# One paced load sequence, half-wide first stages, one PSUM ring and head-pair mask and norm in a sliding-window attention with a highway FFN

## The chip, the core and the metric

The kernel runs on one core of one Trainium2 chip. The metric is device time in microseconds (us) of one execution. Most executions agree within a per cent. Some run slower with a lower granted TensorE clock (the share of full clock that the profile's records show); they are marked as slow and left out of ratios. The span of a profile runs from its first to its last instruction; the device time of the same execution is some 1.7 us longer (213.98 us against 212.3 for the kernel before). Engines are PE (TensorE matmul), PEld (TensorE weight load), DVE (VectorE), ACT (ScalarE), POOL (GpSimd) and SP (SyncE). PSUM is the buffer that TensorE writes its results to; the program cuts it into tiles of one or two banks, a bank being 512 fp32 of each partition here. L394 is a line of the kernel in question, so the same step has another number in another kernel.

## The reference

```python
# q, k, v: (8 batches, 8 heads, 576 tokens, 64), fp32
scores = scale * q @ k.T
mask   = (rel >= 0) & (rel < 128)                 # rel = query position - key position
scores = where(mask, scores - slope[head] * abs(rel), -1e9)
attn   = softmax(scores)
x      = (attn @ v) as (4608 tokens, 512)
H = maximum(x @ w_h, 0)
T = 1 / (1 + exp(-(x @ w_t + b_t)))
out = T * H + (1 - T) * x                          # fp32
```

## The kernel before

Batches go in pairs ("duos", `m` = 0 to 3, two batches `r`). Each duo has two stages: "A" is query and key blocks of 128 tokens 0 and 1, "B" blocks 2, 3 and the tail of 64. For each head there are scores on TensorE, one exponential of 128x1024 on ScalarE, a mask on VectorE, then `pv` on TensorE and the division by the row sum ("norm") on VectorE. A finished stage of all eight heads gives four or five FFN blocks of 128 tokens. One block is: transpose `x`, `h = x @ w_h` (4 matmuls), `z = x @ w_t + b` (4 and a one-row bias matmul), `u = relu(h) - x` on VectorE, `tanh(z/2)` on ScalarE, `t = (tanh + 1)/2` on GpSimd, `u * t` on VectorE, `+ x` on GpSimd, and a store.

GpSimd issues all loads, which narrow fp32 to bf16 on the way. A planner orders all pieces by priorities before the program is emitted, so every engine has a fixed queue.

```python
RING = {"sc": 1, "tr": 2, "av": 2, "a": 1, "z": 1}     # PSUM buffers, one pool each
...
ones1 = cp.tile([1, P], BF16, name="ones1")
bT = cp.tile([1, DM], BF16, name="bT")
...
def mask(u):                                            # one head
    ...
    nc.vector.tensor_tensor(out=o, in0=o, in1=mk, op=ALU.mult)
...
def f_h(st, b):
    xt = XT[st, b]
    pa = ps_a.tile([P, DM], F32, name="pa")
    for c in range(NCK):
        nc.tensor.matmul(out=pa[:], lhsT=xt[:, c, :], rhs=wH[:, c, :], ...)
...
def f_z(st, b):
    xt = XT[st, b]
    pz = ps_z.tile([P, DM], F32, name="pz")
    for c in range(NCK):
        nc.tensor.matmul(out=pz[:], lhsT=xt[:, c, :], rhs=wT[:, c, :], ...)
    nc.tensor.matmul(out=pz[:], lhsT=ones1[:], rhs=bT[:], start=False, stop=True)
```

The softmax here doesn't subtract the row's maximum and nothing guards it: scores larger than these inputs give would overflow.

## Time and profile before

| | before |
|---|---|
| time, median of 3 runs | 212.35 us (212.16 to 212.93) |
| span of the profiled run | 212.3 us |
| TensorE busy | 173.5 us (82%) |
| VectorE, ScalarE, GpSimd busy | 142.4, 124.2, 119.5 us |
| read from HBM | 30.41 MB |

The page's slices are the place to start, since they show when an engine is busy and at which clock; the table of windows then gives numbers to a stretch, and the timeline of that stretch the order of waits.

### The profile page before, as it was taken

Reading aid. Unit: us, or ns where it says so; the run is one execution under the profiler, and the core shown is the slowest. Engines: PE = TensorE matmul, PEld = TensorE weight load, DVE = VectorE, ACT = ScalarE, POOL = GpSimd, SP = SyncE. Lnnn points to the kernel's source line nnn. Section 1 sums busy time; section 2 is a strip of 40 time slices with the busy share of each in tenths; the row PEclk is TensorE's granted clock in tenths of the full one; section 3 lists DMA queues with packets and bytes.
Section 4 is the critical chain, followed back from the end, with each engine's and each line's share of the span. In section 5 each row is a group of like instructions: output and inputs, shape, how many; then the busy total and the mean of one; then the engine's idle time right before and its main releaser. Section 6 shows DMA issues by size and latency. Waiting matters only on the chain.

```text
span 212.3 us, 5013 instructions
## 1 busy us (share of the span) xinstructions
PE 173.5 (82%) x2004; PEld 95.4 (45%) x2004; DVE 142.4 (67%) x308; ACT 124.2 (58%) x161; POOL 119.5 (56%) x137
## 2 busy tenths in 40 slices
PE   0547765995079679999999999999999999997940
PEld 0325443573045422556565445566453455543410
DVE  5626767570094164898886988897789979873550
ACT  2340355657023544889878868877878778824420
POOL 7993493429365395845333896543345564554662
PEclk9999999999555855999999999999999999999995
DMA  5599999999999999994223999322223333324244
GB/s 60 57 195 175 181 173 141 199 172 136 121 196 212 212 165 167 127 199 124 63 54 73 109 114 186 82 54 49 57 70 77 73 79 73 79 51 99 52 98 99
DMA packets 70135, 24.97 MB, mean 118 GB/s; under 512 B 48096, under 2 KB 65504, under 8 KB 70112
## 3 DMA queue, kind: packets, MB, share of 16 engines
q0 software_dynamic: 63328, 15.21, 90.9%
q1 hardware_dynamic: 6784, 9.45, 18.1%
q8 instruction: 15, 0.25, 0.5%
q14 instruction: 8, 0.07, 0.1%
HBM read 30.41 MB, written 9.44 MB: 188 GB/s over the span
## 4 chain that ended last, share of the span: by engine, by line
PE 57%; DMA 25%; POOL 10%; issue 2%; ACT 2%; DVE 1%; POOLq 1%; SPq 0%; ACTq 0%; DVEq 0%
DMA kl<-in_k_dram 19%; PE pz L381 14%; PE pa L364 13%; PE sc L274 8%; PE av L310 8%; DMA va<-in_v_dram 6%; PE pz L383 5%; PE pt L210 4%; PE pt L346 4%; POOL va L104 3%; POOL ql L83 2%; POOL kl L83 1%; POOL ot L403 1%; ACT pt L284 1%; POOL tri L142 1%
## 5 line engine op out<-in xcount | busy, mean ns | idle before, releaser
L284 ACT ACTIVATE pt<-sc,bias 128x1024 bf16<-128x1024 f32 x64 | 71.3, 1115 | 40.9 <-PE sc L274 40.7
L403 POOL TENSOR_TENSOR ot<-uu,x 128x512 f32<-128x512 bf16 x36 | 45.4, 1262 | 21.6 <-DVE uu L399 18.1
L295 DVE TENSOR_TENSOR pt<-pt,mk 128x1024 bf16<-128x1024 bf16 x64 | 49.1, 769 | 6.0 <-ACT pt L284 5.5
L394 POOL TENSOR_SCALAR tt<-tt 128x512 f16<-128x512 f16 x36 | 23.1, 641 | 37.6 <-ACT tt L390 34.7
L310 PE MATMUL av<-va,pt 128*128 128x65 bf16 (+1 forms) x576 | 33.2, 206 | 9.5 <-DVE pt L295 8.0
L364 PE MATMUL pa<-wH,xt 128*128 128x512 bf16 x144 | 39.6, 400 | 1.2 <-ACT xt L356 0.7
L381 PE MATMUL pz<-wT,xt 128*128 128x512 bf16 x144 | 39.8, 401 | 0.2 <-ACT tt L390 0.2
L310 PEld LDWEIGHTS <-pt 128*128 128x128 bf16 (+1 forms) x576 | 25.5, 105 | 23.4 <-DVE pt L295 8.9
L390 ACT ACTIVATE tt<-pz 128x512 f16<-128x512 f32 x36 | 21.6, 599 | 22.0 <-PE pz L383 20.4
L372 DVE SCALAR_TENSOR_TENSOR uu<-pa,x 128x512 bf16<-128x512 f32 x36 | 24.7, 686 | 14.1 <-PE pa L364 14.0
L274 PE MATMUL sc<-qt,kt 64*128 64x256 bf16 (+2 forms) x384 | 28.5, 258 | 5.1 <-ACT pt L284 3.4
L336 DVE TENSOR_TENSOR x<-av,rd 128x256 bf16<-128x256 f32 (+1 forms) x64 | 29.3, 458 | 2.2
L104 POOL DMA_DIRECT2D va<-in_v_dram x20 | 22.2, 1112 | 12.7 <-DMA kl<-in_k_dram 4.2
L399 DVE TENSOR_TENSOR uu<-uu,tt 128x512 bf16<-128x512 bf16 x36 | 16.1, 448 | 17.6 <-POOL tt L394 16.8
L356 ACT COPY xt<-pt 128x512 bf16<-128x512 bf16 x36 | 20.9, 583 | 6.3 <-PE pt L346 6.2
L335 DVE RECIPROCAL rd<-av 128x4 f32<-128x4 f32 (+1 forms) x64 | 11.7, 183 | 15.6 <-PE av L310 15.1
L274 PEld LDWEIGHTS <-kt 64*128 64x128 bf16 x384 | 13.7, 98 | 16.2 <-issue 11.5
L381 PEld LDWEIGHTS <-xt 128*128 128x128 bf16 x144 | 12.3, 101 | 14.4 <-issue 4.3
L346 PE MATMUL pt<-ident,x 128*128 128x128 bf16 x144 | 15.3, 231 | 3.7 <-DVE x L336 3.7
L364 PEld LDWEIGHTS <-xt 128*128 128x128 bf16 x144 | 12.3, 100 | 12.8 <-issue 3.6
L210 PE MATMUL pt<-ident,ql 128*64 128x128 bf16 x256 | 11.8, 244 | 6.9 <-POOL ident L127 5.0
L210 PE MATMUL pt<-ident,kl 128*64 128x128 bf16 x256 | 12.9, 256 | 3.9 <-DMA kl<-in_k_dram 2.2
(42 smaller groups left out, 123.1 us busy)
## 6 DMA issues: line engine op xcount, KB each, us to landing
out_dram<-ot SPq DMA_DIRECT2D x128, 64.0 KB, 1.7
va<-in_v_dram POOLq DMA_DIRECT2D x16, 256.0 KB, 9.3
ql<-in_q_dram POOLq DMA_DIRECT2D x3, 1024.0 KB, 15.6
kl<-in_k_dram POOLq DMA_DIRECT2D x3, 1024.0 KB, 18.1
out_dram<-ot SPq DMA_DIRECT2D x8, 128.0 KB, 2.3
ql<-in_q_dram POOLq DMA_DIRECT2D x2, 384.0 KB, 5.6
kl<-in_k_dram POOLq DMA_DIRECT2D x2, 384.0 KB, 7.9
qtl<-in_q_dram POOLq DMA_DIRECT2D x8, 64.0 KB, 16.5
```

What stands on the lines that cost most here:

```text
L104: nc.gpsimd.dma_start(out=VA[i][0:n, c, :, :, 0:D].rearrange("s r h d -> s (r h) d"), in_=v[2 * m : 2 * m + 2, :, c * P : c * P + n, :].re ...
L210: nc.tensor.transpose(out=pt[r * D : (r + 1) * D, hl * 512 + t * P : hl * 512 + (t + 1) * P], in_=L[:, r, 2 * hp + hl, t * D : (t + 1) * D ...
L274: nc.tensor.matmul(out=sc[:, r, off : off + w], lhsT=KT[i][rows, h, j * P : (j + 1) * P], rhs=rhs, start=True, stop=True,)
L284: nc.scalar.activation(out=pt[:], in_=SC.pop(u)[:], func=ACTF.Exp, bias=BIAS[:, h : h + 1], scale=scale,)
L295: nc.vector.tensor_tensor(out=o, in0=o, in1=mk, op=ALU.mult)
L310: nc.tensor.matmul(out=av[rows, g, :], lhsT=pt[:, r, off : off + w], rhs=va[:, j, r, h, :], start=n == 0, stop=n == len(terms) - 1,)
L336: nc.vector.tensor_tensor(out=x[:, 0:nb, h * D : (h + 1) * D], in0=av[:, 0:nb, 0:D], in1=rd[:, 0:nb].to_broadcast([P, nb, D]), op=ALU.mult,)
L346: nc.tensor.transpose(out=pt[:, c * P : (c + 1) * P], in_=X[st][:, b, c * P : (c + 1) * P], identity=ident[:],)
L364: nc.tensor.matmul(out=pa[:], lhsT=xt[:, c, :], rhs=wH[:, c, :], start=c == 0, stop=c == NCK - 1)
L372: nc.vector.scalar_tensor_tensor(out=uu[:], in0=pa[:], scalar=0.0, in1=X[st][:, b, :], op0=ALU.max, op1=ALU.subtract,)
L381: nc.tensor.matmul(out=pz[:], lhsT=xt[:, c, :], rhs=wT[:, c, :], start=c == 0, stop=False)
L403: nc.gpsimd.tensor_tensor(out=ot[:], in0=UU.pop((st, b))[:], in1=X[st][:, b, :], op=ALU.add)
```

## The change

The intent is to let the loads run as one paced sequence that matches the order in which data is needed, to start work on the first data earlier, to take TensorE's waits on single PSUM buffers away, and to spend less on VectorE.

```diff
+    ORDER = ("abcd", "AB", "AB", "AB")       # duo 0 in four half-wide stages
+    BUFS = {"ps": 4, ...}
-    RING = {"sc": 1, "tr": 2, "av": 2, "a": 1, "z": 1}
+    def ps_tile(dt=F32):                     # every PSUM tile: two banks, ring of four
+        return psp.tile([P, 2, 512 if dt == F32 else 1024], dt, name="ps")
...
-    bT = cp.tile([1, DM], BF16, name="bT")
+    bT = cp.tile([P, DM], BF16, name="bT")   # row 0 is the bias, the rest zero; ones1 alike
...
+    def load_wf():                           # w_h in fp32 by the sync queue, cast on ScalarE
...
     def mask(m, kind, g):                    # now a pair of heads, and so is norm
...
     def f_h(m, kind, b):
-        pa = ps_a.tile([P, DM], F32, name="pa")
+        az = ps_tile()                       # h in bank 0, z in bank 1 of one tile
...
+        if m == 0:
+            qk(0, 0); qk(0, 1); vv(0, 1); w_t, b_t; qk(1); vv(2, 3); tl(); vv(4)
+        else:
+            qk(); tl(); vv(0, 1, 2, 3, 4)
```

(The core of a diff of some 900 lines; the last six lines are written closer than in the kernel.) A half-wide stage covers one key block, so its exponentials are 128x512. The planner also models the loads' pace: in the program GpSimd's loads rotate through eight completion slots, so each waits for the load eight places before it.

## The prediction

> **What bounds the kernel now.** I read the page's slices first, to see where the engines are idle.
>
> ```profile
> PE   0547765995079679999999999999999999997940
> PEclk9999999999555855999999999999999999999995
> DMA  5599999999999999994223999322223333324244
> GB/s 60 57 195 175 181 173 141 199 172 136 121 196 212 212 165 167 127 199 124 63 54 73 109 114 186 82 54 49 57 70 77 73 79 73 79 51 99 52 98 99
> ```
>
> A slice is 5.3 us. From slice 17 on (about 90 us) TensorE is full at full clock; before that it is part idle, and from slice 10 to 15 its clock is halved. The DMA rows are the reverse: full from 10 to 95 us, light afterwards. So there are two regimes: a load-bound first 90 us, and a TensorE-bound rest. The table of ten-microsecond windows puts numbers on it:
>
> ```profile
> 40.00:50.00 10.00, 10.00 (x183) 6.62 (x181) 6.28 (x13) 6.31 (x8) 3.66 (x4) 1.00 2.24 173
> 50.00:60.00 10.00, 1.66 (x34) 1.22 (x31) 1.85 (x5) 2.74 (x3) 5.64 (x8) 0.70 3.48 135
> 60.00:70.00 10.00, 9.54 (x91) 5.19 (x90) 6.12 (x12) 4.13 (x5) 5.77 (x6) 0.50 1.55 208
> 100.00:110.00 10.00, 10.00 (x164) 6.37 (x162) 8.47 (x18) 8.12 (x11) 3.92 (x5) 1.00 0.24 56
> ```
>
> The columns after the width are busy PE, PEld, DVE, ACT, POOL, then clock. All compute collapses at 50 to 60 us. The timeline there says why:
>
> ```profile
> 53.98 0.68 POOL L95 DMA_DIRECT2D ktl<-in_k_dram  x1 [0.87 <-DMA va<-in_v_dram]
> 56.74 0.68 POOL L95 DMA_DIRECT2D ktl<-in_k_dram  x1 [2.08 <-DMA va<-in_v_dram]
> 57.45 0.63 POOL L394 TENSOR_SCALAR tt<-tt 128x512 f16<-128x512 f16 x1
> 58.12 0.42 DVE L399 TENSOR_TENSOR uu<-uu,tt 128x512 bf16<-128x512 bf16 x1 [11.36 <-POOL tt L394]
> 58.46 0.68 DVE L295 TENSOR_TENSOR pt<-pt,mk 128x1024 bf16<-128x1024 bf16 x1
> 59.20 0.82 PE L310 MATMUL av<-va,pt 128*128 128x65 bf16 x11 [6.65 <-DVE pt L295]
> ```
>
> GpSimd issues the loads and also computes one step of the FFN (L394). It sits before a load until an earlier load has landed; L394 stands behind that in its queue, VectorE waits 11.36 us for L394, the mask behind it is late, and TensorE waits 6.65 us for the mask and comes back at half clock. The waits list has the same again at 72 us, where GpSimd waits 6.0 us for a `kl` load. In the full-clock regime I read the timeline of the last blocks, where TensorE does nothing but FFN:
>
> ```profile
> 195.93 1.03 PE L381 MATMUL pz<-wT,xt 128*128 128x512 bf16 x4
> 196.89 0.39 PE L383 MATMUL pz<-bT,ones 1*128 1x512 bf16 x1
> 197.21 0.40 PE L346 MATMUL pt<-ident,x 128*128 128x128 bf16 x4
> 197.44 1.03 PE L364 MATMUL pa<-wH,xt 128*128 128x512 bf16 x4
> 198.31 1.03 PE L381 MATMUL pz<-wT,xt 128*128 128x512 bf16 x4
> ```
>
> Start to start: L364 0.87 us (4 x 0.215), L381 0.96, bias row L383 0.32, transposes 0.23, together 2.38 us a block. L381 and L383 would take 0.86 + 0.215 if they streamed like L364; the one-row bias matmul costs 0.10 us ahead of it and 0.10 after it.
>
> **What the Trainium skill says.** "DMA: Bandwidth & Descriptors", Specifications, gives an HBM limit of about 358 GB/s for a core. The trace agrees: loads narrow fp32 to bf16, so the 173 GB/s written at 40 to 50 us are some 346 GB/s read, and I take the loads as saturated. "TensorE: Matmul & The Clock Gate", Part 1, says that an idle window of some 3.4 us halves the clock; the trace agrees with its 0.50 after the 6.65 us gap (that page's few microseconds of warming don't fit: it stayed cold until about 84 us, over 20 us).[...] "VectorE: DVE Perf Modes", the section on the TRN2 errata, says that the cost of an operation is a fixed part plus elements; its (N+151)/0.96 at two elements a cycle gives 691 ns for the 1024-wide mask, and the timeline has 0.68 to 0.69.
>
> **The change part by part.**
>
> *Loads.* The bytes are the same (30.4 MB read). Order and pace change: first duo by token halves, 8 issues of about 0.78 us from 1.3 us on, so the identity is only made at about 8 us instead of 5 and the first exponential comes at 13 us instead of 10.8 (a loss of 2 to 3 us, but early work waits for `va` anyway). Then second halves, w_t, v, tails; w_h goes by the sync queue with a 2 us cast on ScalarE. Ahead of the first `va` there are 2.1 + 1.05 + 2.1 + 1.05 MB, and it is 0.5 MB: 6.8 MB at 350 GB/s = 19.5 us, plus 2 us start and 2 us landing: 23.5 us (before: 24.25). The rest of duo 0 brings 9.2 MB, 27 to 30 us; duo 1's q and k are 4.2 MB, so 42 us. In before duo 1's last q/k transposes ran at 67 us, because TensorE's queue stood behind the waits above.
>
> *Half-wide first stages.* FFN no longer waits for all of tokens 0 to 255 of eight heads: stage a ends after block 0. In before the first L364 is at 37.9 us; now attention of a and b is waiting masked when `va` lands, and norm of a (4 pairs at 0.6 us) lets FFN start at 27 us. Cost: 32 exponentials of about 0.65 us for 16 of 1.115, +3 us of ScalarE in the first 40 us; twice as many, narrower transposes, +4 us of TensorE.
>
> *Bias with 128 rows of zeros.* Removes 0.2 us a block x 36 = 7.2 us of TensorE.
>
> *Pairs.* Masks: 48 at 0.69 become 24 at (1024+151)/0.96 = 1.22 us: 33.1 to 29.3, 3.8 us saved. Norm: 0.424 and 0.492 us for 256 and 320 elements, slope 1.06 ns, so 512 and 640 take 0.70 and 0.83: per duo 7.3 to 6.1, and 8 reciprocals of 0.18 fewer: 2.6 x 3 = 8 us. VectorE loses 12 of 142 us. It isn't the bound, so this only gives slack.
>
> *PSUM ring.* Scores, transposes, av and FFN tiles share four two-bank slots in place of seven separate buffers. It lets score tiles run ahead of the exponential (in before one `sc` buffer makes a 1.87 us cycle: 0.76 + 1.11), but a slot held by a late tanh or norm stops TensorE whatever comes next. Per duo 47 tiles in 36 us: each may live 4 x 0.77 = 3.1 us; h + z + tanh is 0.86 + 1.08 + 0.6 = 2.5 us at least. I charge 5 to 7% of TensorE's time.
>
> *Sum.* In before, 90 to 180 us holds 22 FFN blocks (88 L364 matmuls), 244 of 384 score matmuls (2.54 duos) and 224 q/k transposes (1.75 duos). With 21.3 us of FFN and 5.3 of transposes a duo, attention is (90 - 52 - 9.3)/2.54 = 11.3, and a duo 37.9 us; four 151 us. So the first 90 us did 37 us worth of work. After: four duos at 36.0, plus 4, 148 us. By 27 us some 13 us of it are done (transposes and scores of the first stages); the other 135 at 93% take 145: TensorE ends at 172. The last block's tanh, two GpSimd and one VectorE steps and the store took 8.5 us behind the last matmul (203.8 to 212.3), and stay. 180.5 us. A second way: duo 1's first exponential at 42.5, three duos at 37.8, then the 28 us from the last exponential to the end, of which eight blocks get 0.2 us shorter plus the better overlap, 25: 181.
>
> **Rivals.**
>
> *GpSimd still blocks FFN.* The built order puts the first `t` steps of the FFN between loads of duo 1, and the later ones behind loads that can only be issued when `ql` and `kl` of duo 1 have landed (some 36 and 42 us). If only three blocks pass before 43 us, TensorE idles, cools, and 8 to 10 us are lost: 190.
>
> *ScalarE becomes the bound.* Per duo: 16 x 1.115 + 9 x (0.583 + 0.6) + 4 x 1.01 + 0.59 = 33.1 us, against 36.0 on TensorE. Near enough to queue, which together with the ring gives a period of 39 to 40: 187. Against it: ScalarE sits at 8.2 tenths in before, with waits of 40.7 us for scores that the ring removes.
>
> *Nothing is lost to the ring.* Period 36: 173 to 175.
>
> *The load-bound phase just moves.* If halves and pacing leave the queue empty, duo 1 comes at 50 instead of 42 us: 188. To be no faster at all, the first 90 us would have to stay as they are.
>
> **Range and chances.** Predicted 180 us. The range of 171 to 192 runs from a frictionless ring to one of the first two rivals in full. For only 208 or more two rivals must add up and the clock must stay low as well: faster 0.93, within 2% 0.04, slower 0.03.
>
> **What would show it.** Right: first FFN matmul near 27 us, duo 1's first exponential near 42 us, no TensorE gap of over 3 us after 30 us and full clock from about 35 us, bias matmuls spaced 0.215 us, pair masks of 1.22 us, PE busy near 165 us or less. Wrong: GpSimd load issues waiting on earlier loads with VectorE behind them at 30 to 60 us; TensorE waiting for tanh or norm (the ring) over 10% of 60 to 160 us; a halved clock after 50 us; ScalarE over 95% busy.

## The result and the profile after

| | before | after |
|---|---|---|
| time, median of the first comparison | 212.64 us (4 runs) | 191.03 us (188.49 to 193.32, 4 runs) |
| ratio of fast runs | | 0.8904 (95% interval 0.8813 to 0.8995) |
| time, repeated later beside the experiments | 213.01 us (11 runs) | 190.9 us (190.04 to 194.48) |
| ratio of fast runs | | 0.9002 (0.895 to 0.9055) |
| TensorE, VectorE busy in the profiled run | 173.5, 142.4 us | 152.3, 136.9 us |
| span of the profiled run | 212.3 us | 188.6 us |

A ratio here is the mean time of one kernel's fast runs over that of the other's of the same rounds, so it is not quite the ratio of the medians. The kernel is about 10% faster. The time lies inside the predicted range, but 11 us above the predicted 180.

The page's slices after the change, 4.7 us each:

```profile
PE   0287769897899888899978889998988899979900
PEclk9999999999999999999999999999999999999995
DMA  4999999999999999999999912043030222433453
GB/s 164 219 183 190 162 128 133 196 190 148 185 178 225 223 197 175 139 200 225 229 172 188 103 41 76 20 99 98 20 87 26 59 70 56 103 81 86 111 128 94
```

The clock row no longer drops: the halved stretch of before is gone. But TensorE is no longer at 9 throughout the second half either; it is between 7 and 9 nearly everywhere. The windows after, with the same columns as those of before (busy PE, PEld, DVE, ACT, POOL, then the clock), show the exchange:

```profile
40.00:50.00 10.00, 8.54 (x167) 5.65 (x167) 8.34 (x16) 6.64 (x11) 7.90 (x8) 1.00 2.45 167
50.00:60.00 10.00, 8.98 (x128) 5.67 (x131) 7.55 (x16) 7.58 (x10) 9.17 (x11) 1.00 1.62 195
60.00:70.00 10.00, 8.88 (x118) 5.49 (x121) 7.70 (x12) 8.00 (x12) 6.57 (x7) 1.00 1.56 217
100.00:110.00 10.00, 8.36 (x105) 5.30 (x104) 7.50 (x12) 7.32 (x11) 3.70 (x5) 1.00 1.26 120
```

At 50 to 60 us TensorE is busy for 8.98 us instead of 1.66 us. At 100 to 110 us it is busy for 8.36 us, where it was full before. So the change wins its time in the load-bound part and gives some back in the part that TensorE bounded.

What it gives back shows in the list of waits (waiting engine and line, releaser, total us, times, longest):

```profile
ACT tt L415 <- DVE uu L400: 38.9, 34, 2.5
DVE uu L400 <- PE ps L410: 26.3, 29, 1.9
```

The times are those of waits that this releaser ended. L415 is the tanh of `z`, L400 is `u` from `h`, L410 is `z`'s bias row. Tanh needs nothing from `u`, and `u` needs nothing from `z`. They wait for each other because `h` and `z` now share one tile, and the program orders accesses by tile: `u` waits until the last write of `z` is done, and tanh waits until `u` has read. The timeline of one block shows what comes of it:

```profile
124.31 0.38 PE L410 MATMUL ps<-bT,ones 128*128 128x512 bf16 x1
...
124.79 0.69 DVE L400 SCALAR_TENSOR_TENSOR uu<-ps,x 128x512 bf16<-128x512 f32 x1 [0.62 <-PE ps L410]
...
125.52 0.60 ACT L415 ACTIVATE tt<-ps 128x512 f16<-128x512 f32 x1 [0.41 <-DVE uu L400]
...
126.17 0.40 PE L299 MATMUL ps<-qt,kt 64*128 64x256 bf16 x4 [0.20 <-ACT tt L415]
```

The bias row is done, then 0.69 us of `u`, then 0.60 us of tanh, and only then do the scores L299 of another head get the slot. From 60 to 160 us TensorE's own list puts three groups of waits, 5.2 us in all, on tanh. The FFN tile lives 0.86 + 1.08 + some 0.1 + 0.69 + 0.60 us and the small gaps, so about 3.4 us in place of the 2.5 us that the prediction took as its least.

The bias row itself is as predicted. From the last blocks:

```profile
170.07 1.03 PE L408 MATMUL ps<-wT,xt 128*128 128x512 bf16 x4
170.93 0.38 PE L410 MATMUL ps<-bT,ones 128*128 128x512 bf16 x1
171.15 1.03 PE L394 MATMUL ps<-wH,xt 128*128 128x512 bf16 x4
```

From L408 to L410 are 0.86 us and from L410 to the next L394 0.22 us, where before they were 0.96 and 0.32.

The first part of the time is late against the prediction. This is the timeline from the landing of duo 1's `kl` to duo 1's first exponential (some lines of other work left out):

```profile
45.07 0.64 PE L248 MATMUL ps<-ident,kl 128*64 128x128 bf16 x16 [0.50 <-DMA kl<-in_k_dram]
45.90 1.01 ACT L273 COPY kt<-ps 128x1024 bf16<-128x1024 bf16 x1
...
48.23 0.64 PE L248 MATMUL ps<-ident,ql 128*64 128x128 bf16 x16
48.70 0.61 PE L248 MATMUL ps<-ident,kl 128*64 128x128 bf16 x16
...
49.24 0.39 PE L299 MATMUL ps<-qt,kt 64*128 64x256 bf16 x4
...
50.98 1.12 ACT L314 ACTIVATE pt<-ps,bias 128x1024 bf16<-128x1024 f32 x1
```

`kl` lands at 45.0 us, not 42. Then TensorE's queue has other work and the second pair of transposes before the first scores (L299, 64x256), and the first exponential of duo 1 starts at 50.98 us, not 42.5.

### The profile page after: what moved, and what is told of

It is laid out like the page before. It is cut to its first block, busy times and chain, and to the rows that moved or that the text cites. A ratio compares the mean times of both kernels' runs of the same rounds, so it can differ in the third digit from the quotient of the medians.

```text
span 188.6 us, 5196 instructions
## 1 busy us (share of the span) xinstructions
PE 152.3 (81%) x2108; PEld 96.1 (51%) x2132; DVE 136.9 (73%) x238; ACT 124.8 (66%) x178; POOL 122.0 (65%) x138
## 4 chain that ended last, share of the span: by engine, by line
PE 30%; DMA 19%; DVE 12%; ACT 12%; issue 11%; POOL 11%; SPq 1%; POOLq 1%; ACTq 0%; DVEq 0%
PE ps L394 11%; PE ps L408 10%; DMA kl<-in_k_dram 9%; DMA va<-in_v_dram 8%; DVE uu L400 7%; ACT pt L314 4%; ACT xt L386 4%; POOL ot L429 4%; DMA out_dram<-ot 3%; PE ps L410 3%; PE ps L248 2%; PE ps L347 2%; DVE pt L324 2%; ACT tt L415 2%; POOL ql L101 2%
## 5 line engine op out<-in xcount | busy, mean ns | idle before, releaser
L314 ACT ACTIVATE pt<-ps,bias 128x1024 bf16<-128x1024 f32 (+1 forms) x80 | 71.9, 951 | 6.2 <-PE ps L299 6.2
L429 POOL TENSOR_TENSOR ot<-uu,x 128x512 f32<-128x512 bf16 x36 | 46.7, 1297 | 22.9 <-DVE uu L424 22.8
L415 ACT ACTIVATE tt<-ps 128x512 f16<-128x512 f32 x36 | 21.5, 597 | 39.0 <-DVE uu L400 38.9
L400 DVE SCALAR_TENSOR_TENSOR uu<-ps,x 128x512 bf16<-128x512 f32 x36 | 24.9, 691 | 29.8 <-PE ps L410 26.3
L324 DVE TENSOR_TENSOR pt<-pt,mk 128x2048 bf16<-128x2048 bf16 (+1 forms) x40 | 43.7, 1099 | 0.7 <-ACT pt L314 0.7
L394 PE MATMUL ps<-wH,xt 128*128 128x512 bf16 x122 | 36.4, 384 | 4.2 <-ACT kt L273 0.6
L408 PE MATMUL ps<-wT,xt 128*128 128x512 bf16 x143 | 36.9, 379 | 0.1
L299 PE MATMUL ps<-qt,kt 64*128 64x256 bf16 (+2 forms) x384 | 27.1, 250 | 6.4 <-ACT tt L415 3.9
L347 PE MATMUL ps<-va,pt 128*128 128x65 bf16 (+1 forms) x576 | 24.9, 198 | 3.7 <-ACT pt L314 1.9
L364 DVE TENSOR_TENSOR x<-ps,rd 128x256 bf16<-128x256 f32 (+3 forms) x40 | 25.5, 638 | 1.4
L408 PEld LDWEIGHTS <-xt 128*128 128x128 bf16 x144 | 14.1, 98 | 17.2 <-issue 0.3
L394 PEld LDWEIGHTS <-xt 128*128 128x128 bf16 x144 | 12.7, 98 | 16.0 <-issue 4.6
L386 ACT COPY xt<-ps 128x512 bf16<-128x512 bf16 x36 | 20.5, 590 | 0.2 <-PE ps L378 0.2
L299 PEld LDWEIGHTS <-kt 64*128 64x128 bf16 x384 | 13.8, 96 | 12.8 <-issue 6.1
L378 PE MATMUL ps<-ident,x 128*128 128x128 bf16 x144 | 14.2, 224 | 2.9 <-ACT tt L415 2.0
```

The costliest lines, as they stand in the source:

```text
L299: nc.tensor.matmul(out=sc[:, r, o + off : o + off + w_], lhsT=KT[i][rows, h, j * P : (j + 1) * P], rhs=rhs, start=True, stop=True,)
L314: nc.scalar.activation(out=PT[m, kind, h // 2][:, h % 2], in_=SC[m, kind, h][:, :, o : o + W], func=ACTF.Exp, bias=BIAS[:, h : h + 1], sca ...
L324: nc.vector.tensor_tensor(out=o, in0=o, in1=mk.to_broadcast([P, 2, rep, W]), op=ALU.mult,)
L347: nc.tensor.matmul(out=av[rows, hl, n * (D + 1) : (n + 1) * (D + 1)], lhsT=pt[:, hl, r, off : off + (D if narrow else P)], rhs=va[:, j, r, ...
L364: nc.vector.tensor_tensor(out=x.rearrange("p b (h d) -> p h b d", h=2), in0=av[:, :, :, 0:D], in1=rd[:, :, 0:nb].to_broadcast([P, 2, nb, D ...
L386: nc.scalar.copy(out=xt[:], in_=TR[m, kind, b][:, 0, 0:512].rearrange("p (c n) -> p c n", c=NCK))
```

## The experiments

All were built from the changed kernel, with the kernel before timed on the same chip in the same rounds. The ratio to before is the common yardstick: 0.9002 for the changed kernel. One hundredth of ratio is 2.1 us. Differences in us below are those of ratios times 212 us, and with the widths of two intervals they are good to some 2 us. The yardstick is open by as much again: the changed kernel was timed twice, with 0.8904 and 0.9002, and not beside the runs from e4_order on. In e1_split, e2_ring3, e4_order, e7_wide, e8_mix, e13_mix0 and e14_first the planner also makes the order of the queues anew, so some part of what they show can be order; in e3_bias1, e5_extra, e6_heads and e10_less the order stays. Two theories stood at the outset. Theory A: TensorE's work and the PSUM ring set the end. Theory B: the moment when duo 1's q and k are there sets it.

**r0_after**, no edit, the yardstick.

> The changed kernel again, on the chip of the next three, as their yardstick. 188 to 193 us as in its four runs so far; it also shows how far it scatters from run to run (before scatters by 0.6%, this one by 2.6%).

Measured: 190.9 us, ratio 0.9002. In its profile the first exponential of duo 1 is at 51.63 us, the last exponential starts at 160.3 us, and the span is 189.3 us.

**e1_split**: `h` and `z` get a one-bank PSUM tile each, and the ring goes from four slots to three to make room.

```diff
-    "ps": 4,
+    "ps": 3, "a": 1, "z": 1,
-        az = ps_tile()
+        az = psa.tile([P, DM], F32, name="pa")      # and psz for z
```

> FFN's two products get a one-bank PSUM tile each (as in the kernel before), the ring of two-bank slots shrinks from 4 to 3. Theory A (the shared two-bank FFN tile makes u wait for z and tanh wait for u, which holds a ring slot some 0.7 us longer and stops TensorE, 7.2 us of waits from 60 to 160 us): the waits of tanh for u (38.9 us) and of u for the bias row (26.3 us) vanish, and 4 to 6 us are gained, about 185 us. Theory B (the shortfall is duo 1's late start at 51 us, set by its k load landing at 45 us): the waits vanish too, but the time stays within 1.5 us of the changed kernel.

Measured: 193.41 us, ratio 0.9112 (0.9051 to 0.9172). The false waits were gone, the end behind the last exponential was 3 us shorter, but duo 1 started at 56.85 us, with the clock at 0.82 between 40 and 50 us. Two things had been changed at once, so it decides nothing by itself.

**e2_ring3**: only the size of the ring is edited (and the planner, which knows it, orders the queues anew).

```diff
-    "ps": 4,
+    "ps": 3,
```

> The ring has 3 slots of two banks in place of 4, nothing else changes; the control of e1. Theory A (slots are short): each tile may live 3 x 0.77 = 2.3 us instead of 3.1, less than the FFN tile's 3.5 us, so 8 to 20 us slower, 198 to 210 us. Theory B (slots are not what limits): within 3 us of the changed kernel.

Measured: 221.52 us, ratio 1.045 (1.0388 to 1.0512), 31 us longer than with four slots and slower than before. The window table for 60 to 160 us:

```profile
60.00:160.00 100.00, 78.62 (x1083) 50.61 (x1098) 63.42 (x100) 65.15 (x82) 49.64 (x50) 0.97 0.99 111
```

TensorE is busy for 78.6 of 100 us. With the FFN's tile in the ring, three slots are far too few, worse than the 8 to 20 us expected. With the same three slots, e1_split is 28 us faster, so giving the FFN's tile two banks of its own, outside the ring, is worth about that much when slots are short.

**e3_bias1**: the one-row bias again.

```diff
-        nc.tensor.matmul(out=az[:, 1, :], lhsT=ones1[:], rhs=bT[:], start=False, stop=True)
+        nc.tensor.matmul(out=az[:, 1, :], lhsT=ones1[0:1, :], rhs=bT[0:1, :], start=False, stop=True)
```

> The bias matmul reads one row again instead of 128 rows of which 127 are zero; undoes that part alone. By the prediction 0.2 us of TensorE for each of 36 blocks: if TensorE is what limits, 5 to 7 us slower than the changed kernel (about 196 us); if TensorE's idle 10% absorbs it, under 2 us.

Measured: 196.83 us, ratio 0.9206 (0.9131 to 0.9281), so 4.3 us longer, of the 7.2 us of TensorE that the 128 rows promised.

**e4_order**: duo 1's q and k are issued ahead of duo 0's tails and last v.

```diff
-            node(key, "POOL", cost, pl + n_, emit, deps, land=land, n=n)
+            late = m == 0 and (key[0] == "tl" or key == ("v", 0, 4))
+            node(key, "POOL", cost, 0.5 * T + 0.01 * n_ if late else pl + n_, emit, deps, land=land, n=n)
```

(and three lines in the planner that keep the order of the rest)

> Duo 1's q and k are issued ahead of duo 0's tails and last v (0.79 MB, some 2.5 us of loading). Theory B (the arrival of duo 1's q and k sets the end, 51.6 + 110 + 28 us): duo 1's first exponential comes 2 to 4 us earlier, near 48, and the whole gets 2 to 4 us shorter, ratio near 0.886. Theory A (TensorE's work and the ring set the end, wherever duo 1 starts): the start may move, the time stays within 1 us of the changed kernel's or gets longer, because duo 0's last stage and its FFN blocks come later; ratio 0.90 or more.

Measured: 199.1 us, ratio 0.938 (0.9299 to 0.9462), 8 us longer. Duo 1's `kl` landed at about 39 us, 6 us earlier, yet its first exponential came at 56.66 us, 5 us later. Data that is there early is of no use when duo 0's last stage, which stands ahead in TensorE's queue, is late: its tails, put later by the edit, made TensorE wait 1.79 us for `ktl` at 44 us. The timeline of that stage shows something else:

```profile
46.76 4.05 DVE L324 TENSOR_TENSOR pt<-pt,mk 128x1024 bf16<-128x1024 bf16 x1 [1.28 <-ACT pt L314]
46.82 1.22 POOL L419 TENSOR_SCALAR tt<-tt 128x512 f16<-128x512 f16 x2
48.00 2.26 POOL L429 TENSOR_TENSOR ot<-uu,x 128x512 f32<-128x512 bf16 x2
```

A mask that takes 0.68 us elsewhere took 4.05 us, and it ended 0.5 us after four GpSimd instructions in a row had ended. TensorE waited 2.23 us for it. Its clock was 0.50 from 48 to 56 us, and had begun to fall before that wait (0.78 at 46 to 48 us). "SBUF — State Buffer", section "SBUF: two separate sides", in the Trainium skill says that VectorE and GpSimd share a pair of ports under an exclusive lock, held for the whole instruction. That fits these lines, and the account of VectorE's time below has more of it from the changed kernel's trace. With a late stage, a blocked mask and a cold clock in one run, e4_order doesn't decide between the theories.

**e5_extra**: two loads of 1 MB that nobody reads, in front of duo 1's q and k.

```diff
+        if m == 0 and c in (2, 3):
+            nc.gpsimd.dma_start(
+                out=wX[:], in_=(moe_w_h, moe_w_t)[c - 2].rearrange("(c p) n -> p c n", p=P))
```

> The opposite: two loads of 1 MB each (w_h and w_t again, into a tile that nothing reads) are put behind duo 0's v of blocks 2 and 3, nothing else moves in any queue. Theory B: at 312 GB/s the 2.1 MB make everything behind them 6.7 us later, duo 1's first exponential at 57 to 58 and the whole 5 to 7 us longer, ratio 0.925 to 0.933. Theory A: TensorE makes up for most of it out of duo 0's FFN backlog; at most 2 us longer, ratio under 0.91.

Measured: 198.54 us, ratio 0.9401 (0.9328 to 0.9473), 8.5 us longer. Its profile (of a run marked slow, span 198.1 us) has TensorE waiting for duo 1's data:

```profile
50.94 1.06 PE L252 MATMUL ps<-ident,kl 128*64 128x128 bf16 x16 [2.95 <-DMA kl<-in_k_dram]
...
58.89 2.13 ACT L318 ACTIVATE pt<-ps,bias 128x1024 bf16<-128x1024 f32 x2
```

`kl` comes about 6 us later, the first exponential 7.3 us later. Later data costs its full delay, and the clock, which was at 0.50 or 0.51 from 50 to 56 us in this run, may have cost the rest: 8.5 us is more than the 5 to 7 of theory B. Theory A as put there, with TensorE making up for the delay, failed this test.

**e6_heads**: mask and norm by single heads again, two instructions in the place of one.

```diff
+        for hl in range(2):
+            o = PT[m, kind, g][:, hl].rearrange("p r (j w) -> p (r j) w", w=W)
...
```

> Mask and norm by single heads again, two instructions in place of each one, at the same places of the queue. Prediction on record (only slack): VectorE gets 11 to 13 us busier, the time stays within 1 us, ratio 0.897 to 0.905. Rival (VectorE is in the loop that holds the PSUM slots and the probabilities): 3 to 6 us longer, ratio 0.915 to 0.93.

Measured: 194.09 us, ratio 0.921 (0.9154 to 0.9266), 4.4 us longer. VectorE was 14 us busier (149.1 us against 135.2). The rival is right: VectorE isn't just slack.

**e7_wide**: duo 0 with the two wide stages of the other duos.

```diff
-    ORDER = ("abcd", "AB", "AB", "AB")
+    ORDER = ("AB", "AB", "AB", "AB")
-        return (0, 1) if ORDER[m][0] == "a" else (None,)
+        return (0, 1) if m == 0 else (None,)
```

> Duo 0 with the two full-wide stages of the other duos; its loads still come by halves. First FFN matmul near 36 in place of 29 us. Prediction's sum (work that is not done before 30 us is added at the end): 4 to 7 us longer, ratio 0.92 to 0.935. Theory B (only duo 1's start counts): duo 1's first exponential within 1.5 us of 51.6, and the time 0 to 2 us longer or even shorter, since 16 exponentials of 0.69 us fewer are needed; ratio 0.895 to 0.91.

Measured: 197.1 us, ratio 0.9349 (0.9294 to 0.9403), 7.4 us longer. The first FFN matmul came at 42.8 us instead of 28.4, TensorE was busy for 6.00 us at 30 to 40 us instead of 8.99, and duo 1 started at 53.2 us. Theory B, by which only that start counts, expected 0 to 2 us. The half-wide stages are a real part of the gain.

**e8_mix**: the same 16 KB of PSUM cut in another way. Scores, q/k transposes and `av` have a ring of three two-bank slots; the FFN's x transposes, `h` and `z` have two one-bank slots.

```diff
-    "ps": 4,
+    "ps": 3, "pf1": 2,
+    def pf_tile(dt=F32):
+        return pfp.tile([P, 512 if dt == F32 else 1024], dt, name="pf")
-        az = ps_tile()                      # h and z in one tile
+        az = pf_tile()                      # one for h, another for z, another for x's transpose
```

> Scores, q/k transposes and av keep a ring of three two-bank slots; the FFN's x transposes, h and z get two one-bank slots of their own (the same 16 KB of PSUM), order made anew by the same rules. The false waits between h and z go, and the FFN no longer holds a slot that scores or av want. If the ring was what TensorE's 10 per cent of idle time came from (prediction's charge of 5 to 7 per cent): 4 to 8 us shorter than the changed kernel, ratio 0.86 to 0.88, mostly in shorter duos or a shorter end. If it is the loads and the order alone: within 2 us, ratio 0.89 to 0.91.

Measured: 184.71 us (183.53 to 186.49), ratio 0.8718 (0.8667 to 0.8769), correct, 6.0 us faster than the changed kernel. Duo 1 starts at 51.61 us, which is where it started with the old layout. The windows of 60 to 160 us, first of the changed kernel (r0_after), then of this one:

```profile
60.00:160.00 100.00, 90.35 (x1251) 58.13 (x1264) 76.56 (x120) 78.23 (x102) 60.83 (x60) 1.00 1.02 120
```

```profile
60.00:160.00 100.00, 93.77 (x1305) 57.56 (x1319) 86.30 (x131) 81.16 (x104) 65.18 (x65) 1.00 1.10 129
```

TensorE's idle time falls from 9.65 to 6.23 us, and more instructions fit in the same 100 us. TensorE's longest group of waits for tanh, in the changed kernel (r0_after) and here:

```profile
PE ps L299 <- ACT tt L415: 3.7, 9, 0.5
```

```profile
PE pf L399 <- ACT tt L421: 0.5, 1, 0.5
```

The gain lies in the duos: from duo 1's first to the last exponential they take 33.8 us each instead of 36.2. The waits of the FFN are now for what it needs, tanh for `z` (L416) and `u` for `h` (L399):

```profile
ACT tt L421 <- PE pf L416: 23.7, 22, 2.2
...
DVE uu L405 <- PE pf L399: 10.8, 11, 2.2
```

**e10_less**: 1.7 MB fewer in front of duo 1's q and k. Its output is wrong, which doesn't matter for the time.

```diff
+        nc.scalar.copy(out=wT[:].rearrange("p c n -> p (c n)"), in_=w_stage())   # w_t isn't loaded
+        nr = 1 if m == 0 and c >= 2 else 2                                       # half of three v blocks
```

> Wrong result on purpose. The counterpart of e5_extra: w_t is not loaded (ScalarE casts w_h twice, one 2 KB load stays in its place) and duo 0's last three v loads bring one of two batch rows (the rest is set to one); 1.7 MB fewer ahead of duo 1's q and k, the order of every queue unchanged. If the arrival of the first 13 MB sets duo 1's start and with it the end (slope of e5_extra: 7.6 us for 2.1 MB): duo 1's first exponential at 46 to 47 and the whole 4 to 6 us shorter, ratio 0.87 to 0.882. If the time only follows delays and earlier data is eaten by work of duo 0 that still has to be done: at most 2 us shorter, ratio 0.89 to 0.90.

Measured: 188.26 us, ratio 0.8908 (0.8845 to 0.8972), 2 us shorter, and duo 1 started at 48.88 us, 2.75 us earlier. The timeline, with L249 the transposes of duo 1:

```profile
42.31 0.38 PE L411 MATMUL ps<-bT,ones 128*128 128x512 bf16 x1
42.62 0.64 PE L249 MATMUL ps<-ident,kl 128*64 128x128 bf16 x16
```

No wait for `kl` stands beside the transposes any more. They come when the FFN block before them in the queue is done. Theory B, which by and large held for delays, fails for earlier data: behind the data limit lies the work of duo 0, less than 3 us away. The end did move about as far as the start (the profiled spans are 186.5 and 189.3 us), so this run speaks about the data, not about the start.

**e13_mix0**: e8_mix with the planner's priorities searched again for that layout.

```diff
-    LOOKS = {"PE": 70, "ACT": 0, "DVE": 109, "POOL": 178, "SP": 159}
+    LOOKS = {'PE': 367, 'ACT': 28, 'DVE': 402, 'POOL': 69, 'SP': 2813}
...
```

(and the twenty shifts of priority in the same way)

> A try at a better version: the PSUM layout of e8_mix with the priorities of the order chosen again for it (the changed kernel's were chosen for one ring of four). 2 to 4 us shorter than e8_mix if order is worth anything there, ratio 0.85 to 0.87; equal to it otherwise.

Measured: 186.55 us, ratio 0.8809 (0.8753 to 0.8864). A miss: it wasn't faster than e8_mix. But with two quite different orders this layout was 4 to 6 us faster than the changed kernel, which speaks for the layout, not the order, as the source of the gain; the old layout with a new order wasn't run.

**e14_first**: only the order, duo 1's first two scores and exponentials moved forward.

```diff
+                up = 8 * T if (m, kind, g) == (1, "A", 0) else 0.0
-                        node(tk, "PE", C[0] * len(hs), tg + (hl - 1.3) * U,
+                        node(tk, "PE", C[0] * len(hs), tg + (hl - 1.3) * U - up,
-                    node(("exp", m, kind, h), "ACT", C[1], tg + (hl - 1.2) * U,
+                    node(("exp", m, kind, h), "ACT", C[1], tg + (hl - 1.2) * U - up,
```

> Only the order: the scores and exponentials of duo 1's first two heads are given a higher priority, so that TensorE takes them before duo 1's second pair of transposes and an FFN block. Duo 1's first exponential comes about 3.5 us earlier, near 48. If the start of duo 1 as such sets the end (all three runs so far that moved it moved the end by the same amount): 3 to 4 us shorter, ratio 0.88 to 0.89. If that start is only where one sees how much of the work before it is done: the time stays within 2 us of the changed kernel's, ratio 0.893 to 0.912.

Measured: 193.47 us, ratio 0.9095 (0.9046 to 0.9144). Duo 1's first exponential came at 49.88 us, 1.75 us earlier and less early than planned, and the whole got 2 us longer, not shorter. After a wait of 1.63 us for a norm TensorE's clock was 0.53 at 44 to 46 us, and it was low again at 50 to 54 us, so part of that is the clock. An earlier start of duo 1 as such brought nothing; because of the clock it is no clean proof that it can't.

## Why the prediction was right or wrong

**Right: two regimes, and GpSimd as the cause of the hole at 50 to 60 us.** The hole and the half clock went away together, and VectorE's waits for GpSimd's `t` step fell from 16.8 to 1.2 us. From 27 to 180 us the list of waits of the changed kernel has no wait of TensorE longer than 0.8 us, and the clock is 1.00 all the while. The first rival, GpSimd blocking the FFN as before, did not come true. Which part of the change closed the hole is not shown: no run puts the old load sequence back alone. The half-wide stages aren't needed for it, since e7_wide has the clock at 1.00 without them. One reading was wrong: before's clock did not stay low until 84 us. It was back at 1.00 at 72 to 74 us and fell again when TensorE was busy for only 0.80 and 0.51 us of two windows of 2 us.

**Right: bias, sizes and first stages.** The bias row's spacing, the pair mask of 1.22 us, the norms of 0.69 and 0.83 us and the first `va` (22.8 us against 23.5) are as worked out. The first FFN matmul came at 29.2 us against 27. e7_wide shows that the half-wide stages are needed for it, and e3_bias1 puts 4.3 us on the bias.

**Wrong: "duo 1's q and k are 4.2 MB, so 42 us".** The 13.4 MB up to there landed at 45.0 us; over some 43 us of loading that is 311 GB/s, not 350. The rate was not one rate: at 36 to 40 us, with q and k under way, the windows have 198 GB/s written, 396 read; at 22.8 to 32.0 us, with v and the tails under way, 129 written, 258 read. Those are read in runs of 64 fp32 values and had been counted at the full rate. "DMA: Bandwidth & Descriptors", Specifications, asks for transfers of at least 512 B for the line rate; these runs of 256 B agree with it, and the prediction didn't apply it. It isn't all: the rate fell from 156 to 119 GB/s written in the course of those loads, which is unexplained. At 350 GB/s the 2.4 MB of these 9.2 us would have taken 6.8 us, so they cost 2.4 us.

**Wrong: the second way's use of that time.** "Duo 1's first exponential at 42.5, three duos at 37.8, then 25" treats the start of duo 1 as a clock from which the rest is counted. Measured, from start to start of exponentials as there, were 51.0, three times 36.2 and 29.0 us, which is 188.6: 8.5 us more, 4.7 less and 4.0 more. It looks as if the late start were the whole miss, and the rival "duo 1 comes at 50 instead of 42 us: 188" hits the time. But e8_mix ends 6 us earlier with the same start, e7_wide starts 1.6 us later and ends 7.4 us later, and with 1.7 MB fewer to load only 2 us come back. Only a delay passed through in full (e5_extra). The rival had the right time for a reason that the runs don't bear out: between 27 and 60 us TensorE was busy for 29.5 of 33 us in the changed kernel, so the late duo 1 was mostly other work done first.

**The sum, term by term.** The first way was 27 + 145 + 8.5 us, with 135 us of TensorE work and 10 us of idle time in the middle. In the profiled run it is 27 + 152.3 + 9.3. In the 152.3 us TensorE is busy for 29.5 + 90.3 + 18.3 = 138.1 us and idle for 14.2. So the miss of 8.1 us in the span is 3.1 us of work, 4.2 us of idle time and 0.8 us at the end. Of the idle time, 3.5 us fall before 60 us and 9.75 us between 60 and 160 us. The 0.8 us at the end is the false wait once more: the last block's tanh waited for `u`, which takes 0.69 us; in e8_mix, without it, the end behind the last matmul takes 8.5 us. What the additional 3.1 us of busy time are made of was not separated; ends of matmuls are modelled in these records. (The sum is one of spans. The time is 1.7 us longer than the span, and the median time 0.7 us longer than that of the profiled run: with them the miss is the 10.5 us from 180.5 to 191.0.)

**Mis-sized: the ring term.** "h + z + tanh is 0.86 + 1.08 + 0.6 = 2.5 us at least" failed because `u` stands in the chain by two false waits, of `u` for `z` and of tanh for `u`: a tile lives about 3.4 us, longer than the 3.1 us of average that four slots allow. The charge of 5 to 7% became 9.75% idle between 60 and 160 us, of which the waits list puts 5.2 us on tanh. e8_mix, which gives the FFN its own slots, takes 6 us back. How much of that is the false dependency and how much the FFN's occupancy of slots was not separated: e1_split took away the first and part of the second, but lost it at duo 1's start.

**Wrong: "this only gives slack".** Undoing the pairs costs 4.4 us. VectorE stands in both chains that hold PSUM slots, through `u` and through the norm, which is the likely way; why 14 us of VectorE time turn into 4.4 us was not followed instruction by instruction. VectorE's busy time fell by 5.5 us between before and after, not by 12. The saving itself came: all masks together fell from 49.1 to 43.7 us, norms with their reciprocals from 41.0 to 33.3. But the 36 products `u * t` rose from 16.1 to 21.0 us. The changed kernel's timeline shows how:

```profile
179.46 1.15 POOL L429 TENSOR_TENSOR ot<-uu,x 128x512 f32<-128x512 bf16 x1
180.02 0.87 DVE L424 TENSOR_TENSOR uu<-uu,tt 128x512 bf16<-128x512 bf16 x1
```

The product ends 0.28 us after GpSimd's addition has ended. Eleven of the 36 products start while a GpSimd instruction of the FFN is running; they take 0.55 to 1.37 us, and every one ends 0.27 to 0.29 us after that instruction. The other 25 take 0.41 to 0.43 us. In before only 2 of 36 start so. That is how blocking for a whole GpSimd instruction, as on the page named at e4_order, would look; the remaining 2.7 us were not taken apart.

**The rival of ScalarE as the bound** found no support: ScalarE was busy for 6.6 to 8.0 us of 10 in the windows shown, and for at most 8.8 in the other windows of ten.

The fastest version is e8_mix, 184.7 us.

## What to carry to other kernels

A shared ring of PSUM slots is paid for by its longest-lived tile, so give tiles that pass through several engines slots of their own, and look in the waits list before two results with different readers share one tile, when waits go by tile. A start time that moves with the end is not yet its cause: shift it by order alone and by data alone, and in both directions, since a delay can pass through in full while an advance meets the next limit (here within 3 us). Half-wide first stages, which start on half of the data, were worth some 7 us here without a byte saved; and loads of small runs are to be counted at a rate measured for them. VectorE instructions that start beside GpSimd's are to be looked at one by one: a mean hides that some take the full length of the other's instruction.

## What the Trainium skill lacked or had wrong

- "SBUF — State Buffer", section "SBUF: two separate sides", has the exclusive lock between VectorE and GpSimd: whichever starts first blocks the other for one instruction. It does not say who gets the ports next when both want them: in e4_order a VectorE mask of 0.68 us was recorded with 4.05 us, across four GpSimd instructions in a row, though the first of these is recorded as starting 0.06 us after the mask.
- "TensorE: Matmul & The Clock Gate", Part 1, puts the cooling at an idle window of some 3.4 us. In e14_first the clock of 44 to 46 us was 0.53 after a gap of 1.63 us between TensorE's records, though in e5_extra, in keeping with the page, it was still 1.00 at 44 to 46 us after a wait of 3.17 us for data. The length of one gap does not decide. The same part gives a warming of a few microseconds, while before's clock stayed at 0.50 from 76 to 84 us (and once before, from 62 to 70 us) with TensorE recorded as busy for 2.00 of every 2 us.
- "TensorE: Matmul & The Clock Gate", Part 2, has no figure for a matmul with one-row weights between full ones: 0.10 us before it and 0.10 us behind it here, and 4.3 us of the whole for 36 of them.
- No page says that a PSUM tile over two banks ties the readers of one bank to the writers of the other where a program's semaphores go by tile: 38.9 us of ScalarE's waits in the changed kernel ended with an instruction whose result it didn't need; with the tiles apart it waited 23.7 us in e8_mix, for `z` itself.
